# A gated mix of decode attention and an MLP: one row of w2 goes to 32 partitions in loads of six, with 29 products fewer on TensorE

## The chip, the cores and the metric

The kernel runs on one core of a Trainium2 chip, all in 32-bit floats. The metric is the device time of one execution in microseconds. Before the change it is 721.7 us, the median of three runs (721.61 to 721.78).

## The reference

One decode step for two sequences (B = 2): a gate mixes attention over a cache of 4096 keys with a two-layer MLP. `x` is 2 x 576, `wq` 576 x 4096 (32 heads of 128), `wo` 4096 x 576, `w1` 576 x 4608, `w2` 4608 x 576.

```python
g = _sigmoid((x * gate_w).sum(-1, keepdims=True))
q = (x @ wq) as (B, 32 heads, 1, 128)
scores = einsum("bhqd,bhkd->bhqk", q, k_cache) * 128 ** -0.5
a = einsum("bhqk,bhkd->bhqd", softmax(scores), v_cache) as (B, 1, 4096) @ wo
b = gelu(x @ w1 + b1) @ w2 + b2
return g * a + (1 - g) * b
```

Nearly all of the 309 MB that are read are the two caches (2 x 134 MB); the four weight matrices are 40 MB. Each weight is used for two rows of x only, so the work is to bring the bytes in and to have each of them consumed in time.

## The kernel before

**The ring.** One SBUF tile of 3 slots, each 64 KB on all 128 partitions, receives every large load in a fixed order: `wq`, `w1`, then for each of 16 units (one sequence, four heads) a K tile and a V tile, and last three slots of weights. `load()` takes the next load from a list and issues it from SP; `load_next(what)` notes that a slot has been read and issues what may follow. The list `LAST` says which rows of `w2` and `wo` are in the last three slots: rows 0 to 27 of `w2` in the first, rows 28 to 35 of `w2` and 0 to 14 of `wo` in the second, the rest of `wo` in the third, in pieces that get smaller. `w2` and `wo` are laid out so that partition p holds rows 36p to 36p + 35 of `w2` (32p to 32p + 31 of `wo`); "row r" below is row r of each partition, and a product with it contracts over the 128 partitions.

**A unit of attention.** VectorE multiplies the K tile by q (`mul`), GpSimd and VectorE sum it up (`red`), VectorE finds the maximum, ScalarE makes the exponentials (`softmax`), and TensorE multiplies them with the V tile (`av`), one unit behind. The K slot is free for the next load when VectorE has read it, the V slot when `av` is done.

**The end.** While the last unit is in work, the rows of `w2` are multiplied with the MLP's hidden values `hg` into an accumulator `acc` (`mlp_out`, `acc_mm`: the columns go in two halves of 288, a product each), then rows of `wo` with the normed attention output `oP` (`wo_out`). A product in 32-bit floats is two passes of TensorE, so the profile counts two matmuls for each. From row `FOLD` of `wo` on, products go to a second accumulator `res` in quarters of 144 columns (`part`), and `acc` is copied to SBUF and folded into `res` by four small products (L473). So the copy of `acc` and the fold are out of the way while the last pieces of `wo` come in. Two copies and one output DMA end the program.

**Row 35 of w2.** Its last 384 columns are loaded apart (`"wx"` in `LAST`): the 128 partitions' pieces go to 16 partitions, eight pieces of 384 columns each, by four loads. Load c goes to partitions c, c + 4, c + 8 and c + 12. Row 35's hidden values are brought to the same places by eight small products (`hxps`, L417), and `mlp_x` multiplies the eight pieces, two products for each.

**The start.** `xps` transposes x by column groups, once for the order of rows in which `w1` is loaded (two chunks of two rows per partition) and once for that of `wq` (four rows). `zps` sums x times the gate's weights by five products. Then come q's products (`qps`) and, behind them, the hidden layer's (`hps`).

Of the kernel before, what the change touches and what calls it, by code (L numbers as in the profile page):

```python
# [10 lines left out]
ALU = mybir.AluOpType  # L11
AX = mybir.AxisListType
P = 128
# [6 lines left out]
def kernel(  # L20
# [14 lines left out]
    nc = tc.nc  # L35
    B, H, SK, DH = k_cache.shape
    D = x.shape[-1]
    F = w1.shape[1]
    NX = D // P
# [9 lines left out]
    ROWS = {"wq": (4,), "w1": (2, 2)}  # L49
# [8 lines left out]
    NF = F // P  # L58
# [5 lines left out]
    SLOTS = 3  # L64

    LAST = (
        (("w2", 0, 14), ("w2", 14, 28)),
        (("w2", 28, 36), ("wx", 0, 1), ("wo", 0, 15)),
        (("wo", 15, 23), ("wo", 23, 27), ("wo", 27, 30), ("wo", 30, 31), ("wo", 31, 32)),
    )  # L70
    FOLD = 23
    SLOT = R * DH
    ALIGN = 512
    FREE0 = 16512
# [24 lines left out]
    kt, vt, wqt, w1t, rows = {}, {}, {}, {}, {}  # L99
# [9 lines left out]
    def load_w(w, rows, c):  # L109
        if c < len(rows):  # L110
            n = rows[c] * w.shape[1]
            lo = sum(rows[:c]) * P
            src = w[lo:lo + rows[c] * P].rearrange("(p r) n -> p (r n)", r=rows[c])
        else:
            n = w.shape[1] // 2
            src = w[NX * P:].rearrange("q (e n) -> (q e) n", e=2)
        t = ring[:, used["w"]:used["w"] + n]
        used["w"] += n
        nc.sync.dma_start(t, src)
        return t  # L120
# [11 lines left out]

    srcs = {"w2": w2.rearrange("(p r) n -> p (r n)", r=NF), "wo": wo.rearrange("(p r) n -> p (r n)", r=32)}

    XE, XC, XW = 4, 4, 384
    XL = D - XW
    XP = XE * XC
    XS = P // XP
    srcx2 = w2.rearrange("(e c s r) n -> c r e s n", e=XE, c=XC, s=XS)[:, NF - 1, :, :, XL:]

    def length(w, a, z):
        return XS * XW if w == "wx" else (z - a) * D - (XW if (w, z) == ("w2", NF) else 0)

    def load_last(m):
        n = sum(length(*q) for q in LAST[m])

        used["e"], used["z"] = len(held) % SLOTS * SLOT + n, (len(held) % SLOTS + 1) * SLOT
        t = slot(n)
        o = 0
        for w, a, z in LAST[m]:  # L150
            if w == "wx":
                xt = t[:XP, o:o + XS * XW]
                rows[w] = xt.rearrange("p (s n) -> p s n", s=XS)
                o += XS * XW
                for c in range(XC):
                    nc.sync.dma_start(xt[c::XC].rearrange("e (s n) -> e s n", s=XS), srcx2[c])
                continue
            if (w, z) == ("w2", NF):
                nc.sync.dma_start(t[:, o:o + length(w, a, z)], srcs[w][:, a * D:z * D - XW])
                for r in range(a, z):  # L160
                    rows[w, r] = t[:, o + (r - a) * D:o + min((r - a + 1) * D, length(w, a, z))]
                o += length(w, a, z)
                continue

            ends = (a * D, a * D + DS, a * D + DS + DO, z * D) if (w, z) == ("wo", 32) else (a * D, z * D)
            for u, v in zip(ends, ends[1:]):
                nc.sync.dma_start(t[:, o:o + v - u], srcs[w][:, u:v])
                o += v - u
            for r in range(a, z):
                rows[w, r] = t[:, o - (z - r) * D:o - (z - r - 1) * D]  # L170

    def temp(n, parts=P):
        t = ring[:parts, used["t"]:used["t"] + n]
        used["t"] += n
        assert used["t"] <= SLOTS * SLOT
        return t
# [30 lines left out]
    xg = temp(D, B + 1)  # L207
# [22 lines left out]
    ident = cp.tile([P, P], F32, name="ident")  # L230
# [29 lines left out]
    nc.gpsimd.memset(xe, 0.0)  # L260
    for e in range(2):
        nc.scalar.copy(xe[:, e, e::2], xg[:, NX * P:])
    def x_rows(rows):
        ends = [sum(rows[:c]) * P for c in range(len(rows) + 1)]
        return [xg[:, lo + r:hi:n] for n, lo, hi in zip(rows, ends, ends[1:]) for r in range(n)]

    srcx = x_rows(ROWS["w1"]) + [xe[:, 0], xe[:, 1]] + x_rows(ROWS["wq"])
    NXT = len(srcx)
    xps = ps_sm.tile([P, NXT, 4], F32, tag="sm", name="xps")
    for c, src in enumerate(srcx):  # L270
# [4 lines left out]
    gT = temp(NX + 1)  # L275
    nc.scalar.copy(gT, xps[:, :NX + 1, B])

    zps = ps_sm.tile([P, B], F32, tag="sm", name="zps")
    for c in range(NX + 1):
        nc.tensor.matmul(zps, gT[:, c:c + 1].to_broadcast([P, P]), xT[:, c, :B], start=(c == 0), stop=(c == NX))  # L280
    gb = cp.tile([P, B], F32, name="gb")
    g1 = cp.tile([P, B], F32, name="g1")
    nc.scalar.activation(gb, zps, AF.Exp, scale=-1.0)  # L283
# [5 lines left out]
    def proj(w, ts, banks, width):  # L289
        full = NG * len(banks) * width  # L290
        for c, n in enumerate(ROWS[w] + (1,)):
            last = c == len(ROWS[w])
            for r in range(n):
                k = sum(ROWS[w][:c]) + r
                for m, ps in enumerate(banks):
                    for j in range(NG):
                        o = (j * len(banks) + m) * width
                        if last:
                            e, o = divmod(o, full // 2)
                            lhs = xT[:, NX + e]  # L300
                        else:
                            o += r * full
                            lhs = xT[:, k if w == "w1" else NX + 2 + k]
                        nc.tensor.matmul(  # L304
                            ps[32 * j:32 * j + 32, :width], lhs, ts[c][:, o:o + width], start=(k == 0), stop=last,
                            skip_group_check=True,
                        )
# [56 lines left out]
    def acc_mm(lhsT, rhs, k, start=False, stop=False, lo=0):  # L364
        m = lhsT.shape[-1]
        hi = lo + rhs.shape[-1]
        for s in range(NS):
            o = 64 * (k % 2) + 32 * s
            u, v = max(lo, s * DS), min(hi, (s + 1) * DS)
            if u < v:  # L370
                nc.tensor.matmul(  # L371
                    acc[o:o + m, u - s * DS:v - s * DS], lhsT, rhs[:, u - lo:v - lo],
                    start=start, stop=stop, skip_group_check=True,
                )
# [39 lines left out]

    hxps = ps_sm.tile([XP, XS, B], F32, tag="sm", name="hxps")
    for s in range(XS):
        nc.tensor.matmul(  # L417
            hxps[:, s], ident.rearrange("p (q s) -> p s q", s=XS)[:, s], hg[:, NF - 1], start=True, stop=True
        )
    hx = cp.tile([XP, XS, B], F32, name="hx")  # L420
    nc.scalar.copy(hx, hxps)

    def mlp_x():
        for s in range(XS):
            acc_mm(hx[:, s], rows["wx"][:, s], s, lo=XL)

    def mlp_out(lo, hi):
        for r in range(lo, hi):
            acc_mm(hg[:, r], rows["w2", r], r)
# [19 lines left out]
    def last_out():  # L449
        res = ps_big.tile([32 * (NC - 1) + B, DO], F32, tag="big", name="res")  # L450
        sums = late(DS)
        nc.scalar.copy(sums, acc)

        def half(t, s):
            if s < 2:
                return t[:, s * DO:(s + 1) * DO]
            return t.rearrange("p (q g c) -> p g q c", q=2, g=2)[:, s - 2]

        def cols(row, s):
            return half(row[:, s // 2 * DS:(s // 2 + 1) * DS], s)  # L460

        def part(r, s):
            nc.tensor.matmul(  # L463
                res[32 * s:32 * s + B], oP[:, :, r], cols(rows["wo", r], s),
                start=r == FOLD, stop=r == 31, skip_group_check=True,
            )

        for r in range(FOLD, 31):
            for s in range(NC):
                part(r, s)  # L470
            if r == FOLD + 3:
                for s in range(NC):
                    nc.tensor.matmul(  # L473
                        res[32 * s:32 * s + B], fold[:, s // 2], half(sums, s),
                        start=False, stop=False, skip_group_check=True,
                    )

        osb = late(D, B)
        cpy = (nc.vector.tensor_copy, nc.scalar.copy)
        for s in range(2):  # L480
            part(31, s)
        for s in range(2):
            cpy[s](osb[:, s * DO:(s + 1) * DO], res[32 * s:32 * s + B])  # L483
        DW = DO // 2
        for q in range(2):
            for s in range(2, NC):
                nc.tensor.matmul(
                    res[32 * s:32 * s + B, q * DW:(q + 1) * DW], oP[:, :, 31], cols(rows["wo", 31], s)[:, q],
                    start=False, stop=True, skip_group_check=True,
                )  # L490
        for s in range(2, NC):
            cpy[s - 2](cols(osb, s), res[32 * s:32 * s + B].rearrange("p (q c) -> p q c", q=2))
        nc.sync.dma_start(out.rearrange("b s d -> (b s) d"), osb)
# [96 lines left out]
    for i in range(N):  # L590
        k = i - 1
# [31 lines left out]
    mlp_out(18, 20)  # L623
    norm_t()
    o_turn(turn)
    mlp_out(20, 24)
    mlp_x()
    mlp_out(24, NF)
    wo_out(0, FOLD)
    last_out()  # L630

# [27 lines left out]
```

## Time and profile before

| | |
|---|---|
| median of three runs | 721.7 us |
| the profiled execution: span from the first to the last instruction | 719.7 us |
| TensorE, matmul passes | 223.4 us busy (31%), 1663 |
| VectorE | 512.0 us busy (71%) |
| GpSimd | 145.0 us busy (20%) |
| ScalarE | 40.0 us busy (6%) |
| DMA from SP's queue | 99.2% of 16 engines' span, 308.55 MB |

The profile gives no other time for its own execution than the span; the 2.0 us between it and the median lie around the first and the last instruction. Engine times are summed over instructions of very different stages. A share of busy time says little by itself: the chain of waits and the windows of a stretch tell what a stage waits for.

### The profile page before, as it was taken

The page shows a single profiled execution, that of the slowest core. Times are in us where ns is not written, and L with a number is a line of the kernel's source. Part 1 is how long each engine was busy: PE and PEld are TensorE (multiplying, and loading weights), DVE is VectorE, ACT ScalarE, POOL GpSimd, SP SyncE. Part 2 cuts the span into 40 slices and gives each one's busy share as a digit, 9 for nine tenths or more (in the row PEclk, how much of TensorE's full clock was granted, in tenths as well). Part 3 has the DMA queues.
Part 4 walks back from the last instruction along what each step waited for, and adds up shares of the span by engine and source line. Part 5 has one row for each costly group of instructions (what it writes and reads, how often), then busy time and mean ns, then how long its engine had stood idle before and what let it go on. Part 6 is the DMA issues. An engine that isn't in the chain of part 4 may idle for free.

```text
span 719.7 us, 3913 instructions
## 1 busy us (share of the span) xinstructions
PE 223.4 (31%) x1663; PEld 66.1 (9%) x1663; DVE 512.0 (71%) x137; ACT 40.0 (6%) x156; POOL 145.0 (20%) x35
## 2 busy tenths in 40 slices
PE   0675022040514050404133140405060503214198
PEld 0321000010101010101000010101010100000024
DVE  0004969779695969596969879696959695988910
ACT  0110010100001010101010100001010101010000
POOL 2000130404050403022040404040403122040400
PEclk9967557565757575655756575757565665657588
DMA  9999999999999999999999999999999999999997
GB/s 408 412 443 434 426 444 419 455 416 455 416 444 428 426 441 430 438 430 444 430 434 426 441 430 437 431 433 437 437 434 441 423 431 437 430 441 431 420 424 308
DMA packets 7126, 308.83 MB, mean 429 GB/s; under 512 B 810, under 2 KB 1342, under 8 KB 1604
## 3 DMA queue, kind: packets, MB, share of 16 engines
q1 hardware_dynamic: 7060, 308.55, 99.2%
q8 instruction: 13, 0.21, 0.1%
q14 instruction: 5, 0.04, 0.0%
q10 hardware_dynamic: 48, 0.03, 0.0%
HBM read 308.57 MB, written 0.00 MB: 429 GB/s over the span
## 4 chain that ended last, share of the span: by engine, by line
DMA 45%; DVE 35%; PE 17%; ACT 1%; issue 1%; ACTq 0%; POOL 0%; DVEq 0%; POOLq 0%
DMA ring<-in_A_k_cache_dram 39%; DVE ring L512 19%; PE av L551 10%; DVE s L517 10%; DVE s L518 5%; DMA ring<-in_B_w_dram 4%; PE acc L371 3%; DMA ring<-in_gate_w_dram 3%; PE oall L568 2%; PE qps L304 1%; DVE avs L562 1%; PE res L463 0%; ACT p L537 0%; DVE m L522 0%; PE zps L280 0%
## 5 line engine op out<-in xcount | busy, mean ns | idle before, releaser
L512 DVE TENSOR_TENSOR ring<-ring,q 128x16384 f32<-128x16384 f32 x16 | 275.6, 17225 | 110.1 <-DMA ring<-in_A_k_cache_dram 110.1
L516 POOL TENSOR_TENSOR ring<-ring 128x3968 f32<-128x3968 f32 x16 | 137.0, 8565 | 491.3 <-DVE ring L512 491.3
L551 PE MATMUL av<-ring,p 128*32 128x512 f32 x1024 | 141.6, 715 | 167.6 <-ACT p L537 167.6
L517 DVE TENSOR_REDUCE s<-ring 128x66 f32<-128x8448 f32 x16 | 143.2, 8953 | 1.3
L568 PE MATMUL oall<-avs,pick 128*64 128x512 f32 x16 | 14.8, 1028 | 195.1 <-DVE avs L562 167.7
L518 DVE TENSOR_REDUCE s<-ring 128x62 f32<-128x3968 f32 x16 | 68.4, 4277 | 0.1
L551 PEld LDWEIGHTS av<-ring,p 128*32 128x32 f32 x1024 | 36.0, 129 | 278.8 <-issue 220.6
L537 ACT ACTIVATE p<-s,bs 32x128 f32<-32x128 f32 x64 | 25.5, 398 | 479.9 <-DVE bs L531 478.7
L352 PE MATMUL qb<-qm,spread 64*128 64x512 f32 x8 | 8.3, 1138 | 71.4 <-POOL qm L348 71.4
L395 DVE TENSOR_TENSOR ring<-hps,ring 128x384 f32<-128x384 f32 x3 | 1.7, 559 | 32.2 <-PE hps L304 32.0
L371 PE MATMUL acc<-ring,hg 128*2 128x288 f32 (+1 forms) x142 | 14.4, 561 | 25.3 <-DMA ring<-in_B_w_dram 25.3
L568 PEld LDWEIGHTS oall<-avs,pick 128*64 128x64 f32 x16 | 2.2, 196 | 201.9 <-DVE avs L562 201.9
L284 DVE TENSOR_SCALAR gb<-gb 128x2 f32<-128x2 f32 x1 | 0.2, 169 | 24.4 <-ACT gb L283 24.4
L483 DVE COPY ring<-res 2x144 f32<-2x144 f32 x1 | 0.3, 296 | 19.3 <-PE res L463 19.3
L304 PE MATMUL hps<-ring 128*32 128x384 f32 x120 | 12.8, 596 | 0.0
L562 DVE TENSOR_TENSOR avs<-av,selr 128x512 f32<-128x512 f32 x8 | 5.5, 682 | 10.1 <-PE av L551 10.1
L348 POOL TENSOR_TENSOR qm<-qall,mine 64x512 f32<-64x512 f32 x4 | 4.1, 1035 | 40.3 <-ACT qall L331 40.3
L537 ACT ACTIVATION_READ_ACCUMULATOR p<-s,bs 32x1 f32 x64 | 11.8, 184 | 0.0
L304 PE MATMUL qps<-ring 128*32 128x512 f32 x80 | 10.7, 697 | 0.0
L271 PE MATMUL xps<-ident,ring 3*128 3x3 f32 x10 | 1.5, 254 | 23.8 <-DMA ring<-in_gate_w_dram 22.8
L352 PEld LDWEIGHTS qb<-qm,spread 64*128 64x128 f32 x8 | 2.0, 308 | 74.5 <-POOL qm L348 74.5
L354 ACT COPY q<-qb 128x512 f32<-128x512 f32 x4 | 2.3, 585 | 106.3 <-PE qb L352 106.3
(88 smaller groups left out, 79.5 us busy)
## 6 DMA issues: line engine op xcount, KB each, us to landing
ring<-in_B_w_dram SPq DMA_DIRECT2D x2, 4608.0 KB, 34.3
ring<-in_B_w_dram SPq DMA_DIRECT2D x2, 4032.0 KB, 28.6
ring<-in_A_wo_dram SPq DMA_DIRECT2D x1, 4320.0 KB
ring<-in_A_wo_dram SPq DMA_DIRECT2D x1, 2304.0 KB, 22.4
ring<-in_B_w_dram SPq DMA_DIRECT2D x1, 2112.0 KB
ring<-in_B_w_dram SPq DMA_DIRECT2D x1, 1152.0 KB
ring<-in_A_wo_dram SPq DMA_DIRECT2D x1, 1152.0 KB
ring<-in_A_wq_dram SPq DMA_DIRECT2D x1, 1024.0 KB
```

What stands on the lines that cost most here:

```text
L304: nc.tensor.matmul(ps[32 * j:32 * j + 32, :width], lhs, ts[c][:, o:o + width], start=(k == 0), stop=last, skip_group_check=True,)
L348: nc.gpsimd.tensor_mul(t, qall.unsqueeze(1).to_broadcast([NO, NQ, DH]), mine[:, u[0]:u[-1] + 1].unsqueeze(2).to_broadcast([NO, NQ, DH]),)
L352: nc.tensor.matmul(ps, spread, t.rearrange("p u d -> p (u d)"), start=True, stop=True)
L371: nc.tensor.matmul(acc[o:o + m, u - s * DS:v - s * DS], lhsT, rhs[:, u - lo:v - lo], start=start, stop=stop, skip_group_check=True,)
L512: nc.vector.tensor_mul(kt[i], kt[i], qs[i].unsqueeze(1).to_broadcast([P, R, DH]))
L516: nc.gpsimd.tensor_add(t[:, :, :DH2], t[:, :, :DH2], t[:, :, DH2:])
L517: nc.vector.tensor_reduce(st[i][:, HALVED:], kt[i][:, HALVED:], AX.X, ALU.add)
L518: nc.vector.tensor_reduce(st[i][:, :HALVED], t[:, :, :DH2], AX.X, ALU.add)
L537: nc.scalar.activation(p[w, :, e * RB:(e + 1) * RB], st[i][w].rearrange("p (t c) -> p t c", c=RB), AF.Exp, bias=bias[i][w], accum_out=rs[w ...
L551: nc.tensor.matmul(ps[32 * j:32 * j + 32], p[:, 32 * t + EB * (1 - half):32 * t + EB * (1 - half) + 32], vt[i][:, RB * t:RB * (t + 1)].rea ...
L562: nc.vector.tensor_mul(t, avs[i].rearrange("p (r d) -> p r d", d=DH), selr.unsqueeze(2).to_broadcast([P, RB, DH]))
L568: nc.tensor.matmul(oall, pick[:, NO - G - i * G:2 * NO - G - i * G], avs[i].rearrange("p r d -> p (r d)"), start=(i == 0), stop=(i == N // ...
```

## The change

Row 35 of `w2` goes whole (576 columns) to 32 partitions: partition q gets four pieces, those of w2's partitions q, q + 32, q + 64 and q + 96, at a step of 768 columns. It is loaded by six loads of up to six neighbouring partitions, three behind rows 0 to 13 and three behind rows 14 to 21, all in the first slot; rows 22 to 34 move to the second. The hidden values of row 35 take four small products instead of eight, and `mlp_x` eight full-width products instead of sixteen narrow ones. The second accumulator begins at row 27 of `wo`, and the fold stands behind row 29. At the start, both weights are taken in the order of four rows per partition, so x is transposed once (6 transposes instead of 10), and the gate's sum is a multiply and a reduction on VectorE and one product.

```diff
     LAST = (
-        (("w2", 0, 14), ("w2", 14, 28)),
-        (("w2", 28, 36), ("wx", 0, 1), ("wo", 0, 15)),
+        (("w2", 0, 14), ("wx", 0, 3), ("w2", 14, 22), ("wx", 3, 6)),
+        (("w2", 22, 35), ("wo", 0, 15)),
...
-    FOLD = 23
+    FOLD = 27
...
-            lo = sum(rows[:c]) * P
-            src = w[lo:lo + rows[c] * P].rearrange("(p r) n -> p (r n)", r=rows[c])
+            lo = sum(rows[:c]) * w.shape[1]
+            src = w[:NX * P].rearrange("(p r) n -> p (r n)", r=NX)[:, lo:lo + n]
...
-    XE, XC, XW = 4, 4, 384
-    XL = D - XW
-    XP = XE * XC
+    XE, XP = 6, 32
     XS = P // XP
-    srcx2 = w2.rearrange("(e c s r) n -> c r e s n", e=XE, c=XC, s=XS)[:, NF - 1, :, :, XL:]
+    XT = 768
+    srcx2 = w2.rearrange("(s q r) n -> q s r n", q=XP, s=XS)[:, :, NF - 1]
...
-                for c in range(XC):
-                    nc.sync.dma_start(xt[c::XC].rearrange("e (s n) -> e s n", s=XS), srcx2[c])
...
+                for c in range(a, z):
+                    u, v = c * XE, min((c + 1) * XE, XP)
+                    nc.sync.dma_start(rows[w][u:v], srcx2[u:v])
...
-    srcx = x_rows(ROWS["w1"]) + [xe[:, 0], xe[:, 1]] + x_rows(ROWS["wq"])
+    srcx = [xg[:, r:NX * P:NX] for r in range(NX)] + [xe[:, 0], xe[:, 1]]
...
-    for c in range(NX + 1):
-        nc.tensor.matmul(zps, gT[:, c:c + 1].to_broadcast([P, P]), xT[:, c, :B], start=(c == 0), stop=(c == NX))
+    xz = temp((NX + 1) * B).rearrange("p (b c) -> p b c", b=B)
+    nc.vector.tensor_mul(
+        xz, xT[:, :NX + 1, :B].rearrange("p c b -> p b c"), gT.unsqueeze(1).to_broadcast([P, B, NX + 1])
+    )
+    zs = temp(B)
+    nc.vector.tensor_reduce(zs, xz, AX.X, ALU.add)
+    nc.tensor.matmul(zps, ones.to_broadcast([P, P]), zs, start=True, stop=True)
...
-        nc.tensor.matmul(
-            hxps[:, s], ident.rearrange("p (q s) -> p s q", s=XS)[:, s], hg[:, NF - 1], start=True, stop=True
-        )
+        nc.tensor.matmul(hxps[:, s], ident[:, s * XP:(s + 1) * XP], hg[:, NF - 1], start=True, stop=True)
...
-            acc_mm(hx[:, s], rows["wx"][:, s], s, lo=XL)
+            acc_mm(hx[:, s], rows["wx"][:, s], s)
...
-            if r == FOLD + 3:
+            if r == FOLD + 2:
...
-    mlp_out(20, 24)
+    mlp_out(20, 22)
     mlp_x()
-    mlp_out(24, NF)
+    mlp_out(22, NF - 1)
```

SP's queue, from the last V tile's load to the first of `wo` (names are out<-in, sizes partitions x elements), before:

```order
L130 DMA ring<-in_A_v_cache_dram 128x16384
L167 DMA ring<-in_B_w_dram 128x8064 x2
L159 DMA ring<-in_B_w_dram 128x4224
L156 DMA ring<-in_B_w_dram 4x8x384 x4
L167 DMA ring<-in_A_wo_dram 128x8640
```

and after:

```order
L130 DMA ring<-in_A_v_cache_dram 128x16384
L163 DMA ring<-in_B_w_dram 128x8064
L157 DMA ring<-in_B_w_dram 6x4x576 x3
L163 DMA ring<-in_B_w_dram 128x4608
L157 DMA ring<-in_B_w_dram 6x4x576 x2
L157 DMA ring<-in_B_w_dram 2x4x576
L163 DMA ring<-in_B_w_dram 128x7488
L163 DMA ring<-in_A_wo_dram 128x8640
```

The small loads moved from behind the second slot's `w2` into the first slot, between and behind its two parts, and part of the first slot's rows moved to the second.

TensorE, from the end of the attention (`op_t` turns its output) to the end of the program, before (the pairs of `hx` products of 96 and 288 columns, eight in all, are cut to the last):

```order
L441 MATMUL op_t<-ring 128x64
L371 MATMUL acc<-ring,hg 2x288 x8
L371 MATMUL acc<-ring,hx 2x96
L371 MATMUL acc<-ring,hx 2x288
L371 MATMUL acc<-ring,hg 2x288 x22
L371 MATMUL acc<-ring,hg 2x192
L371 MATMUL acc<-ring,oP 2x288 x46
L463 MATMUL res<-ring,oP 2x144 x16
L473 MATMUL res<-ring,fold 2x144 x4
L463 MATMUL res<-ring,oP 2x144 x18
L487 MATMUL res<-ring,oP 2x72 x4
```

and after:

```order
L436 MATMUL op_t<-ring 128x64
L368 MATMUL acc<-ring,hg 2x288 x4
L368 MATMUL acc<-ring,hx 2x288 x8
L368 MATMUL acc<-ring,hg 2x288 x26
L368 MATMUL acc<-ring,oP 2x288 x54
L458 MATMUL res<-ring,oP 2x144 x12
L468 MATMUL res<-ring,fold 2x144 x4
L458 MATMUL res<-ring,oP 2x144 x6
L482 MATMUL res<-ring,oP 2x72 x4
```

The sixteen `hx` products became eight, four rows of `wo` moved from `res` to `acc`, and the fold now has only six quarter products and the last four behind it.

More of the change, by code (lines that the diff above doesn't have):

```diff
@@ L133 @@
     srcs = {"w2": w2.rearrange("(p r) n -> p (r n)", r=NF), "wo": wo.rearrange("(p r) n -> p (r n)", r=32)}
-    XE, XC, XW = 4, 4, 384
-    XL = D - XW
-    XP = XE * XC
+    XE, XP = 6, 32
     XS = P // XP
-    srcx2 = w2.rearrange("(e c s r) n -> c r e s n", e=XE, c=XC, s=XS)[:, NF - 1, :, :, XL:]
+    XT = 768
+    srcx2 = w2.rearrange("(s q r) n -> q s r n", q=XP, s=XS)[:, :, NF - 1]
     def length(w, a, z):
-        return XS * XW if w == "wx" else (z - a) * D - (XW if (w, z) == ("w2", NF) else 0)
+        if w == "wx":
+            return XS * XT if a == 0 else 0
+        return (z - a) * D
     def load_last(m):
@@ L151, in load_last @@
             if w == "wx":
-                xt = t[:XP, o:o + XS * XW]
-                rows[w] = xt.rearrange("p (s n) -> p s n", s=XS)
-                o += XS * XW
-                for c in range(XC):
[L156 to L161, printed above, removed]
+                if a == 0:
+                    rows[w] = t[:XP, o:o + XS * XT].rearrange("p (s n) -> p s n", s=XS)[:, :, :D]
+                for c in range(a, z):
+                    u, v = c * XE, min((c + 1) * XE, XP)
+                    nc.sync.dma_start(rows[w][u:v], srcx2[u:v])
                 o += length(w, a, z)
@@ L262 @@
         nc.scalar.copy(xe[:, e, e::2], xg[:, NX * P:])
-    def x_rows(rows):
-        ends = [sum(rows[:c]) * P for c in range(len(rows) + 1)]
-        return [xg[:, lo + r:hi:n] for n, lo, hi in zip(rows, ends, ends[1:]) for r in range(n)]
-    srcx = x_rows(ROWS["w1"]) + [xe[:, 0], xe[:, 1]] + x_rows(ROWS["wq"])
+    srcx = [xg[:, r:NX * P:NX] for r in range(NX)] + [xe[:, 0], xe[:, 1]]
     NXT = len(srcx)
@@ L302, in proj @@
                             o += r * full
-                            lhs = xT[:, k if w == "w1" else NX + 2 + k]
+                            lhs = xT[:, k]
                         nc.tensor.matmul(
```

## The prediction

> **What bounds the kernel now.** I read the page first: its header, the row of DMA busy shares in 40 slices, and the chain of work that ended last.
>
> ```profile
> span 719.7 us, 3913 instructions
> DMA  9999999999999999999999999999999999999997
> DMA packets 7126, 308.83 MB, mean 429 GB/s; under 512 B 810, under 2 KB 1342, under 8 KB 1604
> DMA 45%; DVE 35%; PE 17%; ACT 1%; issue 1%; ACTq 0%; POOL 0%; DVEq 0%; POOLq 0%
> ```
>
> The span is 2.0 us below the median of the three runs (721.7 us); the profile gives no other time of its own, so every sum is made on the span and the 2.0 us are added back. All 16 DMA engines are at 90% or more in every slice but the last: 308.83 MB at 429 GB/s are 719.9 us, the span itself. The chain names TensorE and VectorE for half of the time, but it only walks through whoever consumed a tile last. So I read the end closely: first the windows (last two columns: mean busy share of the 16 DMA engines, GB/s), then the timeline of the last 2 us.
>
> ```profile
> 691.00:695.00 4.00, 4.00 (x44) 1.11 (x36) 1.21 (x4) 0.16 (x1) 0.00 (x0) 1.00 1.05 439
> 700.00:712.00 12.00, 12.00 (x134) 5.11 (x126) 0.00 (x0) 0.00 (x0) 0.00 (x0) 0.68 0.97 415
> 713.10:713.70 0.60, 0.60 (x15) 0.19 (x8) 0.00 (x0) 0.00 (x0) 0.00 (x0) 1.00 0.84 332
> 713.70:714.30 0.60, 0.60 (x20) 0.39 (x16) 0.00 (x0) 0.14 (x1) 0.00 (x0) 1.00 0.81 329
> 714.30:714.90 0.60, 0.60 (x28) 0.47 (x18) 0.00 (x0) 0.27 (x1) 0.00 (x0) 1.00 0.63 231
> 714.90:715.50 0.60, 0.60 (x21) 0.31 (x15) 0.00 (x0) 0.00 (x0) 0.00 (x0) 1.00 0.63 228
> 715.50:716.10 0.60, 0.60 (x28) 0.47 (x20) 0.00 (x0) 0.00 (x0) 0.00 (x0) 1.00 0.47 152
> 716.10:716.40 0.30, 0.30 (x14) 0.08 (x4) 0.00 (x0) 0.00 (x0) 0.00 (x0) 1.00 0.21 63
> 716.40:716.70 0.30, 0.30 (x10) 0.11 (x7) 0.00 (x0) 0.00 (x0) 0.00 (x0) 1.00 0.00 0
> ...
> 714.93 0.09 PEld L473 LDWEIGHTS res<-ring,fold 128*2 128x2 f32 x2
> 715.25 0.84 PEld L463 LDWEIGHTS res<-ring,oP 128*2 128x2 f32 x32 [0.23 <-DMA ring<-in_A_wo_dram]
> 716.32 0.10 PEld L463 LDWEIGHTS res<-ring,oP 128*2 128x2 f32 x4 [0.23 <-DMA ring<-in_A_wo_dram]
> 716.55 0.28 PEld L487 LDWEIGHTS res<-ring,oP 128*2 128x2 f32 x8
> ```
>
> Two things are to be seen. The engines do not stop together: the share falls from 0.84 to 0.00 over 3.3 us, so some have done their part by 713.7 and the last work until 716.4. And TensorE, behind until 714.93, waits for wo's last pieces at 715.25 and 716.32. The end is therefore the landing of wo's last piece on the slowest engine, with some 3.3 us of products, copies and output write behind it that the change leaves alone. The idle share below 1 from 713.1 to 716.4, 0.6 x (0.16 + 0.19 + 0.37 + 0.37 + 0.53) + 0.3 x 0.79, is 1.2 us: no rebalancing of engines that moves the same bytes can bring more than that.
>
> **TensorE's part.** The groups of the last 30 us, two pieces of the timeline, one of the chain of waits (zps) and one of SP's timeline:
>
> ```profile
> L371 PE MATMUL acc<-ring,oP 128*2 128x288 f32 x92 | 6.5, 406 | 0.0
> L463 PE MATMUL res<-ring,oP 128*2 128x144 f32 x68 | 3.0, 286 | 0.0
> ...
> 698.94 4.01 PE L371 MATMUL acc<-ring,hx 16*2 16x96 f32 x32
> 702.88 0.66 PE L371 MATMUL acc<-ring,hg 128*2 128x288 f32 x4
> ...
> 25.71 2.26 PE zps L280 x10
> 36.96 0.33 SPq L130 DMA_DIRECT2D ring<-in_A_k_cache_dram  x1
> ```
>
> A product is two passes, so x32 are 16 products. Row 35's slices: 16 products from 698.94 to 702.88, 3.94 us; 8 of them at full width remain, about 2 us by halving; the product with 192 columns goes too (0.25 us by the same pace). wo's rows 23 to 26: 16 products less at 3.0/34 = 0.09 us, 8 more at 6.5/46 = 0.14 us, 0.3 us less. In sum 2.5 us less work for TensorE, all ahead of the waits at 715.25 and 716.32 and hidden by them. Against it, the products that fold in the accumulator move behind row 29, past the wait at 715.25. They are 8 passes at 3.0/68 = 0.04 us, 0.35 us, where 0.23 us are idle before 716.32; the 0.1 us that may be left is absorbed by the next pieces of wo. Sum: 0.
>
> At the start 4 transposes, 4 products of the gate and 4 of hxps go, and VectorE gets a multiply and a reduction, for which TensorE waits ahead of q's products. Four fifths of 2.26 us are 1.8 us less, two short VectorE operations some 0.5 us more; so the first K load, at 36.96, goes out about 1.3 us earlier, and even if it went out later the queue ahead of it is full (the second and third slices read 9). w1 is fetched in the same pieces of two rows, from places twice as far apart. No row prices that; between 0 and the slowest slice's pace I take 0, since the same number of bytes per piece is fetched.
>
> **The queue's part, which decides.** An engine's pace is 429/16 = 26.8 KB per us. Row 35's 192 columns leave the loads over all 128 partitions: 8 partitions x 768 B = 6.1 KB per engine, -0.23 us. The small loads grow from 4 x 48 KB to 288 KB, so the bytes in all stay as they are and only their places change. If a partition's bytes stay on one engine (taken, since a load of few partitions has no finer share that any row shows), four engines had 48 KB each, 1.83 us; now a partition gets 9 KB, 0.34 us, four engines carry five of these (1.72 us) and two carry six (2.06 us). Net of the -0.23 us: 0.0 us for the two, -0.3 us for two others that had such loads before, +1.5 us for two that had none, -0.23 us for the ten others. If the bytes spread over all engines, all get 0. So by bytes alone the last landing moves by 0.0 to -0.23 us.
>
> But the loads also change where engines write. Before, a load stepped by 4 partitions: partitions c, c+4, c+8, c+12. Now six neighbours are written by six engines at once. The window 691 to 695 shows the four old loads in passing at 439 GB/s, no slower than the stretch behind them: with a step of 4 they disturb nobody. No row shows engines writing neighbours at one time, so I bound it. Low end: 0, an engine's pace is its own. [...] The engines are not quite in step: they are spread over 3.3 us at the end, and a load reached alone costs only its 0.34 us. I take the middle, 2.7 us: of the two ends the nearer row is the spread, and it is of the length of the loads themselves. The loads stand some 8 to 20 us into the first slot's transfers, on full queues, so nothing later makes up for it. With 0.2 us of it met by what these engines shed, the last landing is 2.5 us later: 721.7 + 2.5 = 724.2 us.
>
> [...]
>
> **SP's queue and the second slot.** SP's timeline, and one of its waits (us in total, times, longest):
>
> ```profile
> 651.58 3.76 SPq L167 DMA_DIRECT2D ring<-in_B_w_dram  x2
> 681.63 0.33 SPq L159 DMA_DIRECT2D ring<-in_B_w_dram  x1
> 682.39 2.84 SPq L156 DMA_DIRECT2D ring<-in_B_w_dram  x4
> 689.74 0.33 SPq L167 DMA_DIRECT2D ring<-in_A_wo_dram  x1
> ...
> SPq L167 <- DMA ring<-in_B_w_dram: 5.9, 2, 4.6
> ```
>
> The second slot is issued at 681.63, when VectorE is done with the last K tile; that does not move. Ahead of it the first slot now holds 22 rows of w2, not 28: 6 x 2,304 B x 128 = 1.77 MB, 4.1 us less in every engine. The issue at 689.74 ended the 4.6 us wait, for rows 14 to 27 to land, so the slowest engine's queue reached 8.1 us past 681.63 and now reaches 4.0 us past it, and the fastest, 3.3 us ahead, 0.7 us. The six small loads add 1 us to their own engines there. An empty queue took 1.0 us from issue to first packet:
>
> ```profile
> 0.74 0.87 SPq L119 DMA_DIRECT2D ring<-in_A_wq_dram  x2
> ...
> 0.70:1.70 1.00, 0.00 (x0) 0.00 (x0) 0.00 (x0) 0.00 (x0) 0.97 (x1) 1.00 0.00 0
> 1.70:2.20 0.50, 0.00 (x0) 0.00 (x0) 0.00 (x0) 0.00 (x0) 0.42 (x3) 1.00 4.25 1442
> ```
>
> So the earliest engines may idle for about 0.3 to 1 us, and they have that to spare at the end. Term: 0, high end +1 us. The small loads cost SP 0.6 to 0.8 us each to issue; two more fit into the wait before 681.63.
>
> **Rivals.** (1) Engines do not share a way: only bytes count, 721.7 - 0.2 = 721.5 us. For it: no row shows a slow-down between engines. Against it: all 16 together sit at one ceiling slice after slice (429 GB/s), which fits a limit at the destination as well as one in the engine. From 1.4 us of meeting upwards it loses to the forecast; between 0.2 and 1.4 us the result is within the bound too. (2) TensorE's chain is what counts and 29 products fewer shorten it: at most 2.5 us, 719.2 us; but only if the landings came earlier by as much, and balance can give 1.2 us, so 720.5 us. Against it are the waits at 715.25 and 716.32. (3) The two engines that are new to the small loads are among the last: the last landing comes 1.5 us later, 723.2 us; they would have to be of the few that work past 715.5 (share 0.47). (4) The queue runs dry for the slow engines as well: an issue would have to take 4 us and more to reach them; 721.7 + 1.5 = 723.2 us.
>
> **How the numbers follow.** The forecast, meeting with more than 1.4 us, has 0.55, its own range 723.2 to 725.6 us; meeting with less 0.10; rival 1 0.28; rival 2 0.02; rivals 3 and 4 together 0.05. A difference under 0.2% (1.4 us) is about what a measurement of this kernel cannot tell from no change. Faster: 0.02 of rival 2 and 0.01 for an unforeseen gain, 0.03; slower: 0.55 + 0.04 (the half of the 0.05 that tops the bound, and unforeseen losses), 0.59; same: 0.38. The range goes from rival 1's 721.4 us to 725.5 us, short of the 727.0 us of engines fully in step.
>
> **What would show it.** In the windows of the stretch 677 to 690 us the GB/s should dip below 400 while the busy share stays near 1, and the last landing (the last wait of the weight loads for wo, now near 716.6) should come near 719. Right on TensorE: longer idle time before the last products. Wrong if the small loads pass at 420 GB/s or more and the share falls to zero by 716.5: then rival 1 holds. A dip of the share itself near 682 to 684 us would be rival 4.

## The result: 724.2 us, 0.35% slower, and the profile after

The changed kernel takes 724.24 us (median of five runs, 723.88 to 724.70), the kernel before beside it 721.70 us (721.61 to 721.86): a ratio of 1.0035, 95% interval 1.0023 to 1.0047. So it is slower by 2.5 us, with 54 matmul passes fewer. From the page:

```profile
span 722.6 us, 3811 instructions
PE 213.5 (30%) x1609; PEld 59.4 (8%) x1609; DVE 512.3 (71%) x139; ACT 40.0 (6%) x156; POOL 144.9 (20%) x35
DMA packets 7141, 308.82 MB, mean 427 GB/s; under 512 B 826, under 2 KB 1230, under 8 KB 1620
DMA 49%; DVE 35%; PE 14%; ACT 1%; issue 1%; ACTq 0%; DVEq 0%; POOL 0%; POOLq 0%
```

The bytes are the same to 0.01 MB, and TensorE is busy 9.9 us less. The chain of work that ended last has lost three points of TensorE and gained four of DMA. Now the end, in the same windows as before (from 713.1 us; last two columns: mean busy share of the 16 DMA engines, GB/s):

```profile
713.10:713.70 0.60, 0.60 (x16) 0.29 (x11) 0.00 (x0) 0.00 (x0) 0.00 (x0) 1.00 0.99 415
713.70:714.30 0.60, 0.60 (x18) 0.47 (x12) 0.00 (x0) 0.00 (x0) 0.00 (x0) 1.00 0.94 390
714.30:714.90 0.60, 0.60 (x16) 0.43 (x10) 0.00 (x0) 0.00 (x0) 0.00 (x0) 1.00 1.00 405
714.90:715.50 0.60, 0.60 (x12) 0.09 (x2) 0.00 (x0) 0.00 (x0) 0.00 (x0) 1.00 0.93 363
715.50:716.10 0.60, 0.10 (x6) 0.05 (x8) 0.00 (x0) 0.00 (x0) 0.00 (x0) 1.00 0.73 271
716.10:716.70 0.60, 0.60 (x12) 0.28 (x16) 0.00 (x0) 0.00 (x0) 0.00 (x0) 1.00 0.60 230
716.70:717.30 0.60, 0.51 (x12) 0.00 (x0) 0.00 (x0) 0.03 (x1) 0.00 (x0) 1.00 0.51 175
717.30:717.90 0.60, 0.00 (x0) 0.00 (x0) 0.00 (x0) 0.38 (x1) 0.00 (x0) 1.00 0.19 66
717.90:718.50 0.60, 0.40 (x16) 0.36 (x20) 0.00 (x0) 0.00 (x0) 0.00 (x0) 1.00 0.10 35
718.50:719.10 0.60, 0.60 (x31) 0.52 (x23) 0.00 (x0) 0.00 (x0) 0.00 (x0) 1.00 0.07 22
719.10:719.70 0.60, 0.60 (x28) 0.43 (x16) 0.00 (x0) 0.00 (x0) 0.00 (x0) 1.00 0.01 3
```

And the timeline of TensorE's weight loads there (start, us, what, in brackets the idle time before it):

```profile
713.30 1.69 PEld L368 LDWEIGHTS acc<-ring,oP 128*2 128x2 f32 x32 [0.25 <-DMA ring<-in_A_wo_dram]
716.05 0.59 PEld L368 LDWEIGHTS acc<-ring,oP 128*2 128x2 f32 x16 [1.06 <-DMA ring<-in_A_wo_dram]
718.10 0.60 PEld L458 LDWEIGHTS res<-ring,oP 128*2 128x2 f32 x24 [1.45 <-DMA ring<-in_A_wo_dram]
```

The windows hold two losses of different kinds. First, everything is later: from 714.3 to 714.9 us all engines still work (1.00) where before 0.63 did. The share summed over these windows is 0.6 x 6.07 = 3.64 us, against 0.6 x 3.38 + 0.3 x 0.21 = 2.09 us in the rows of before. So the average engine ends 1.55 us later, with no byte more in all, and the engines without small loads are among these: six of 16 alone would be a share of 0.375. Second, the tail is longer: from 717.9 to 719.1 us the share is 0.10 and then 0.07, and one engine of 16 is 0.0625. One engine works alone for about 1 us, and the last landing moves from about 716.5 to about 719.1 us, by 2.6 us. TensorE, the weight loads show, now waits 1.06 and 1.45 us for `wo` where it waited 0.23 us twice.

The stretch in which the small loads are fetched, before and then after:

```profile
677.00:680.00 3.00, 0.00 (x0) 0.00 (x0) 2.88 (x2) 0.00 (x0) 0.28 (x1) 0.50 1.02 441
680.00:685.00 5.00, 4.78 (x52) 1.61 (x56) 2.29 (x4) 1.96 (x8) 0.00 (x0) 0.63 1.00 432
685.00:690.00 5.00, 5.00 (x56) 1.44 (x48) 0.00 (x0) 0.00 (x0) 0.00 (x0) 1.00 0.96 410
```

```profile
677.00:680.00 3.00, 0.02 (x3) 0.02 (x6) 2.88 (x2) 0.00 (x0) 0.29 (x1) 0.50 0.99 382
680.00:685.00 5.00, 5.00 (x52) 1.66 (x56) 2.30 (x4) 1.96 (x8) 0.00 (x0) 0.61 1.03 387
685.00:690.00 5.00, 5.00 (x54) 1.44 (x48) 0.00 (x0) 0.06 (x1) 0.00 (x0) 1.00 1.00 361
690.00:700.00 10.00, 8.49 (x83) 2.46 (x79) 2.63 (x9) 0.37 (x1) 0.00 (x0) 0.88 1.00 428
```

The share stays at 1 while the rate falls to 361 to 387 GB/s: packets take longer. That is 3 x 59 + 5 x 45 + 5 x 49 = 647 KB short of before, 1.5 us of the whole core at 429 GB/s.

### The profile page after: what moved, and what is told of

Read it like the earlier page. It is cut to its first block, busy times and chain, and to the rows that moved or that the text cites. A ratio compares the mean times of both kernels' runs of the same rounds, so it can differ in the third digit from the quotient of the medians.

```text
span 722.6 us, 3811 instructions
## 1 busy us (share of the span) xinstructions
PE 213.5 (30%) x1609; PEld 59.4 (8%) x1609; DVE 512.3 (71%) x139; ACT 40.0 (6%) x156; POOL 144.9 (20%) x35
## 4 chain that ended last, share of the span: by engine, by line
DMA 49%; DVE 35%; PE 14%; ACT 1%; issue 1%; ACTq 0%; DVEq 0%; POOL 0%; POOLq 0%
DMA ring<-in_A_k_cache_dram 39%; DVE ring L507 19%; DVE s L512 10%; PE av L546 9%; DVE s L513 5%; DMA ring<-in_A_wo_dram 4%; DMA ring<-in_B_w_dram 4%; DMA ring<-in_gate_w_dram 3%; PE oall L563 2%; PE qps L301 1%; PE acc L368 1%; DVE avs L557 1%; ACT p L532 0%; DVE m L517 0%; DVE mt L522 0%
## 5 line engine op out<-in xcount | busy, mean ns | idle before, releaser
L546 PE MATMUL av<-ring,p 128*32 128x512 f32 x1024 | 135.9, 691 | 171.5 <-ACT p L532 171.5
L368 PE MATMUL acc<-ring,hg 128*2 128x288 f32 x140 | 13.9, 548 | 24.9 <-DMA ring<-in_B_w_dram 24.9
L368 PE MATMUL acc<-ring,oP 128*2 128x288 f32 x108 | 8.7, 475 | 2.9 <-DMA ring<-in_A_wo_dram 2.9
```

The source lines that it names most:

```text
L368: nc.tensor.matmul(acc[o:o + m, u - s * DS:v - s * DS], lhsT, rhs[:, u - lo:v - lo], start=start, stop=stop, skip_group_check=True,)
L546: nc.tensor.matmul(ps[32 * j:32 * j + 32], p[:, 32 * t + EB * (1 - half):32 * t + EB * (1 - half) + 32], vt[i][:, RB * t:RB * (t + 1)].rea ...
```

## Experiments

Three causes are told apart. **N**: small loads to neighbouring partitions slow each other. **Q**: large loads are issued so late that queues run dry. **L**: one of the two engines that are new to the small loads is a late one and decides by its bytes. The experiments ran in three groups of four, each on one chip with the kernel before beside it, at 721.73, 721.68 and 721.78 us.

**The parts that the prediction put at 0.** The kernel before with only the start part of the change (its diff as it stands) and the later fold:

```diff
-    FOLD = 23
+    FOLD = 27
...
-            if r == FOLD + 3:
+            if r == FOLD + 2:
```

> The kernel before with only the start part of the change (w1's pieces, 4 transposes and 4 products fewer, VectorE's multiply and sum) and the later fold (row 27, added behind row 29); row 35 and its loads as before. All theories, and the prediction's terms of 0 for these parts: 721.5 to 721.9 us. If the work that TensorE loses mattered, 720.5 us; if the fold behind row 29 or the wait for VectorE cost something, 722.0 us or more.

Measured: 721.92 us (721.75 to 721.99, 11 runs), ratio 1.0000 (0.9992 to 1.0009). These parts neither cost nor bring anything that can be measured; the whole loss belongs to row 35, its loads and the shorter first slot that goes with them.

**Neighbours alone.** The kernel before, its four small loads sent to four neighbours each:

```diff
-    srcx2 = w2.rearrange("(e c s r) n -> c r e s n", ...)[:, NF - 1, :, :, XL:]
+    srcx2 = w2.rearrange("(c e s r) n -> c r e s n", ...)[:, NF - 1, :, :, XL:]
...
-                    nc.sync.dma_start(xt[c::XC].rearrange("e (s n) -> e s n", s=XS), srcx2[c])
+                    nc.sync.dma_start(xt[c * XE:(c + 1) * XE].rearrange("e (s n) -> e s n", s=XS), srcx2[c])
```

> The kernel before (721.7 us), but load c of row 35's slices goes to partitions 4c to 4c + 3 instead of c, c + 4, c + 8, c + 12; bytes, engines, queue places and products are the same. N: slower, by 1 to 5 us (four loads that take up to 1.8 us each where 0.46 us were due), 722.7 to 727 us, with a dip of the GB/s in the window 691 to 695 us (439 before). Q and L: 721.7 us, no change.

Measured: 722.87 us (722.71 to 723.39, 11 runs), ratio 1.0016 (1.0008 to 1.0025). The same bytes in the same number of issues, on as many engines, cost 1.1 us more. In the windows:

```profile
690.00:695.00 5.00, 5.00 (x52) 1.57 (x48) 0.71 (x2) 0.43 (x1) 0.00 (x0) 1.00 1.04 410
717.30:717.90 0.60, 0.60 (x22) 0.20 (x12) 0.00 (x0) 0.00 (x0) 0.00 (x0) 1.00 0.08 23
```

The loads pass at 410 GB/s (436 in the same window before), and an engine is at work past 717.3 us. N is shown. The expectation's 1.8 us for each of the four loads, 7.3 us where 1.83 us were due, was the author's estimate for four engines that go one after another; no run shows it, and 1.1 us came. That the place of writing is what counts stays an inference: neighbours are also fetched from places closer together, and no run parted the two.

**The loads left out.** The changed kernel without the six loads and their products (`pass` in place of the `dma_start`, no `mlp_x()`).

> The changed kernel without the six small loads and without the eight products on them; row 35 of w2 is left out of the result, and 288 KB are not read. The first slot is as short as in the changed kernel, so its queues are as dry. N and L: the whole loss goes and 0.2 us more, 721.3 to 721.6 us, GB/s near 420 in the window 685 to 690 us. Q: 722.5 us and more, and the dip stays.

Measured: 721.92 us (721.53 to 724.08, 11 runs), ratio 1.0007 (0.9998 to 1.0015). So by the medians the loads are 2.3 of the 2.5 us. But the windows, of an execution of 723.1 us, warn:

```profile
677.00:680.00 3.00, 0.00 (x0) 0.00 (x0) 2.90 (x2) 0.00 (x0) 0.58 (x1) 0.50 0.89 381
680.00:685.00 5.00, 4.94 (x48) 1.58 (x52) 2.58 (x4) 1.96 (x8) 0.00 (x0) 0.57 1.02 395
685.00:690.00 5.00, 5.00 (x57) 1.53 (x52) 0.00 (x0) 0.00 (x0) 0.00 (x0) 1.00 0.93 387
```

The rate dips to 381 to 395 GB/s there without any small load. In two of the rows the share is 0.89 and 0.93: the shortened first slot leaves early engines idle, as Q says. In the middle row it is 1.02 at 395 GB/s, so packets are slow there too. By the median this costs 0.4 us against the 721.5 us that the shed bytes alone would give. It also brings a wider scatter: the slowest execution, at 724.08 us, takes as long as the changed kernel. The dip in this stretch, which the prediction named as its mark, is therefore no proof of N.

**The loads moved elsewhere.** Two runs take the first slot as before and put the six loads behind. In the first they stand behind `w2`'s row 34, ahead of `wo`:

```diff
-        (("w2", 0, 14), ("wx", 0, 3), ("w2", 14, 22), ("wx", 3, 6)),
-        (("w2", 22, 35), ("wo", 0, 15)),
+        (("w2", 0, 14), ("w2", 14, 28)),
+        (("w2", 28, 35), ("wx", 0, 6), ("wo", 0, 15)),
```

> The changed kernel, but with the first slot as before (w2's rows 0 to 27) and all six small loads in the second slot behind rows 28 to 34, where the kernel before has its four. Q: the loss by dry queues goes, 722.5 to 723 us. N and L: the loss stays, 724.0 to 724.8 us, and the dip of the GB/s moves to the stretch behind 690 us.

Measured: 724.31 us (723.72 to 724.79, 6 runs), ratio 1.0034 (1.0022 to 1.0046). In the second they stand behind `wo`'s row 14 as well (`("w2", 28, 35), ("wo", 0, 15), ("wx", 0, 6)`, and `mlp_x()` between `wo_out(0, 15)` and `wo_out(15, FOLD)`):

> The changed kernel with w2's rows 0 to 27 in the first slot, and in the second rows 28 to 34, then wo's rows 0 to 14, and the six small loads of 6 neighbours last; TensorE takes the 8 products of row 35 behind wo's row 14. So no large load is issued late: wo's first piece follows at 682, not at 689.5 as where six small loads stood ahead of it, and the first slot is as long as before. Theory Q in its wider form (a large load issued when the engines are about to run out slows all of them): 722.8 to 723.5 us, what is left being neighbours and the late engine. Theories N and L without Q: 724.0 to 724.6 us, as the changed kernel.

Measured: 724.76 us (724.65 to 725.01, 5 runs), ratio 1.0040 (1.0026 to 1.0054). The rows of the windows, of the first and then of the second:

```profile
690.00:695.00 5.00, 4.58 (x48) 1.31 (x40) 1.60 (x4) 0.00 (x0) 0.00 (x0) 1.00 1.20 377
695.00:700.00 5.00, 3.14 (x27) 0.96 (x27) 1.03 (x5) 0.00 (x0) 0.00 (x0) 0.68 0.88 344
```

```profile
690.00:695.00 5.00, 5.00 (x50) 1.43 (x43) 0.69 (x1) 0.43 (x1) 0.00 (x0) 1.00 1.04 447
695.00:700.00 5.00, 3.50 (x50) 1.54 (x52) 1.95 (x8) 0.00 (x0) 0.00 (x0) 1.00 1.01 432
700.00:705.00 5.00, 2.09 (x32) 0.69 (x24) 0.00 (x0) 0.00 (x0) 0.00 (x0) 1.00 1.02 342
705.00:712.00 7.00, 5.86 (x64) 2.19 (x68) 0.00 (x0) 0.00 (x0) 0.00 (x0) 0.76 0.96 368
```

The dip goes where the loads go: to 690 to 700 us, then to 700 to 712 us, where before moved 412 and 416 GB/s. In the second run that is 5 x 70 + 7 x 48 = 686 KB, 1.6 us of the whole core, at a share near 1. Its first slot is as long as before. The first piece of the third slot was issued later, at 694.4 us and not at 688.1, but the share shows no empty queue, so dry queues have no part in its 3.0 us.

**A late issue alone.** In the first of these two runs SP issued `wo`'s first piece at 689.5 us instead of 685.3, since it waited for an earlier transfer to land. So the kernel before was given six issues for its four small loads, same bytes and places:

```diff
-                    nc.sync.dma_start(xt[c::XC]..., srcx2[c])
+                    for u, v in ((0, XS // 2), (XS // 2, XS)) if c < 2 else ((0, XS),):
+                        nc.sync.dma_start(xt[c::XC]...[:, u:v], srcx2[c][:, u:v])
```

> The kernel before, with two of its four small loads cut into halves by columns: same bytes on the same engines and partitions, a step of 4, only six issues for four. wo's first piece then waits for the landing of w2's rows 14 to 27 and is issued near 689.5 us and not at 685.3. Theory Q in its wider form: 722.2 to 723.0 us, with GB/s below 400 in 690 to 700. Theories N and L: 721.7 us, no dip.

Measured: 721.63 us (721.50 to 721.95, 11 runs), ratio 0.9997 (0.9988 to 1.0006). One row of SP's timeline, then two of the windows:

```profile
689.72 0.34 SPq L170 DMA_DIRECT2D ring<-in_A_wo_dram  x1
```

```profile
690.00:695.00 5.00, 5.00 (x52) 1.53 (x48) 0.69 (x1) 0.15 (x1) 0.00 (x0) 1.00 1.03 426
695.00:700.00 5.00, 3.50 (x46) 1.52 (x46) 1.95 (x8) 0.28 (x1) 0.00 (x0) 0.85 1.03 444
```

The issue is late, and no dip and no loss follow: Q in its wider form, that a late issue alone costs time, falls. Where a late issue does cost is shown by accident. Row 35 on five engines, in seven loads (`slice(c, 30, 6) if c < 6 else slice(30, 32)`, in the second slot):

> Row 35 on five engines: six small loads of 5 partitions a step of 6 apart and one of 2, in the second slot; 54 KB for three engines and 63 KB for two of the old four. Theory L: if the late engine is the sixth, it is out of it, and 721.7 to 722.2 us; if it is the fifth, 722.8 us or more, as with six engines. Theory N: 721.5 to 721.9 us. This is also the smallest change that could give a version as fast as the kernel before with eight products of full width.

Measured: 725.45 us (724.87 to 727.76, 5 runs), ratio 1.0058 (1.0045 to 1.0071). A seventh issue made SP wait once more. Again one row of SP's timeline and two of the windows:

```profile
695.44 0.82 SPq L163 DMA_DIRECT2D ring<-in_A_wo_dram  x2
```

```profile
690.00:695.00 5.00, 5.00 (x52) 1.45 (x44) 1.11 (x4) 0.00 (x0) 0.00 (x0) 1.00 0.62 249
695.00:700.00 5.00, 3.49 (x35) 1.01 (x35) 1.53 (x6) 0.41 (x1) 0.00 (x0) 0.77 0.86 298
```

Here the share itself falls to 0.62: engines are empty. That is what rival 4 would look like, and the changed kernel shows nothing of the kind. About five engines and lateness this run says nothing.

**A step of 5.** The changed kernel, partition c + 5e in place of 6c + e (`q = slice(c, 30, 5) if c < 5 else slice(30, 32)`), first in the places of the change, then in the second slot:

> The changed kernel (724.24 us), but a small load goes to partitions c, c + 5, ... c + 25 instead of six neighbours (the last one to 30 and 31 as before): same engines, bytes, places in the queue. Theory N (engines of one load that write neighbouring partitions hold each other and the rest up): most of a slow-down of about 1.7 us goes, 722.4 to 723.0 us, and the GB/s of the window 685 to 690 us rise from 361 towards 420. Theory Q (the second slot is issued too late for the shortened first slot, queues run dry): nothing changes, 724.2 us. Theory L (one of the two engines that are new to the small loads is a late one): by itself also 724.2 us; together with N 722.8 us is left.

Measured: 723.43 us (five runs: 723.12, 723.43, 723.43, 725.02, 725.19), ratio 1.0032 (1.0020 to 1.0045).

> The changed kernel with both suspects but one taken away: six small loads to partitions a step of 5 apart (no neighbours) and behind w2's rows 28 to 34 in the second slot (no dry queue); the two engines that are new to small loads keep them. Theory N alone (neighbours are the loss): 721.5 us, as before. Theory L (one of the two new engines is late into w2 and decides by its bytes): 722.8 to 723.1 us, with the share of DMA time at 0.06 to 0.1 for the last 0.6 us or more. Theory Q (dry queue): 721.5 us.

Measured: 723.81 us (723.35, 723.51, 723.81, 725.58, 725.61), ratio 1.0037 (1.0025 to 1.0050). Neither differs from the changed kernel beyond the intervals, so both expectations missed: a step of 5 doesn't take the loss away. Both runs fall into two groups some 2 us apart, and the profiled executions (723.43 and 723.81 us) belong to the lower ones. In these, the share summed over the windows from 713.1 us on, as for the changed kernel, puts the average engine 0.85 and 0.98 us behind before, not 1.55: a part of the slow-down went.

A possible reason for the rest, only argued: the engines aren't in step (at the end of the kernel before they stop over 3.3 us, while a small load takes 0.34 us by the prediction's estimate), so one engine's load may meet another load of the engine that writes beside it. Why four loads with a step of 4, as in the next run, escape this, no run shows.

**Eight and four engines.** Row 35 in four loads with a step of 4, in the second slot: first on 32 partitions and eight engines (`q = slice(c, XP, 4)`, four loads), then on 16 partitions and four engines (`XE, XP = 4, 16`, `XT = 576`, so eight pieces per partition; rows 13 and 14 of `wo` move to the third slot).

> Row 35 on eight engines: four small loads of 8 partitions, a step of 4 apart, in the second slot; 36 KB per engine, so four engines get 1.15 us net that they had not, and the four old ones shed 0.7 us. Theory N: no neighbours, 721.5 us or below. Theory L: the late one is among the four new ones, 722.5 to 722.8 us, 0.2 to 0.4 us below six engines. Only the fullest engine counts: 721.2 us.

Measured: 722.53 us in two groups: 721.27, 721.33, 721.37, 721.53, and seven runs from 722.38 to 722.86; ratio 1.0007 (0.9999 to 1.0016).

> The whole of row 35 on four engines: four small loads of 4 partitions, a step of 4 apart, 18 KB each (8 products of 16 partitions), in the second slot; wo's rows 13 and 14 move to the third slot. The four engines get 72 KB where before they had 48, net of the 6 KB that every engine sheds +0.7 us for these; no neighbours and no engine new to small loads. Theory N: nothing beside the bytes, so 721.5 to 722.4 us, by how late the four are. Theory L: 722.4 us, since these four end within 0.6 us of the last engine before; still faster than six engines at a step of 5 though the loads per engine are larger. If neither counts and only the number of bytes in the fullest engine does (72 KB here, 54 KB with six), this is slower than six engines: 723.5 us or more against 722.9.

Measured: 722.57 us (722.47 to 722.76, 11 runs), ratio 1.0013 (1.0004 to 1.0022). Windows of the run on eight engines (its profiled execution belongs to the higher group), then of that on four:

```profile
690.00:695.00 5.00, 4.40 (x48) 1.42 (x36) 1.78 (x5) 0.00 (x0) 0.00 (x0) 1.00 1.06 443
695.00:700.00 5.00, 3.81 (x27) 1.13 (x27) 0.86 (x5) 0.41 (x1) 0.00 (x0) 0.64 1.00 431
715.50:716.10 0.60, 0.10 (x4) 0.10 (x8) 0.00 (x0) 0.07 (x1) 0.00 (x0) 1.00 0.35 111
716.10:716.70 0.60, 0.60 (x24) 0.53 (x23) 0.00 (x0) 0.00 (x0) 0.00 (x0) 1.00 0.06 23
716.70:717.30 0.60, 0.60 (x26) 0.51 (x20) 0.00 (x0) 0.00 (x0) 0.00 (x0) 1.00 0.05 15
```

```profile
716.10:716.70 0.60, 0.60 (x24) 0.52 (x28) 0.00 (x0) 0.00 (x0) 0.00 (x0) 1.00 0.23 76
716.70:717.30 0.60, 0.60 (x30) 0.50 (x20) 0.00 (x0) 0.00 (x0) 0.00 (x0) 1.00 0.23 55
```

The eight-engine run moves the same 288 KB as the change and shows no dip (443, 431): with a step of 4, N is gone. What is left is L, though no execution of the lower group was profiled. In the lower group the 721.4 us are those of bytes alone (721.7 less the shed 0.23). In the higher one a single engine (0.06, 0.05) works about 1.2 us past the others, and the groups lie 1.3 us apart (medians 722.68 and 721.35), which is 36 KB at 26.8 KB per us. On four engines 0.23 x 16 = 3.7 engines work to the end together: there the four carriers' 72 KB decide, in every run alike, at the 722.4 us that bytes give.

**Packet by packet.** The trace holds the size and the time of every packet, though no view prints them. One piece of row 35 is one packet. Undisturbed it takes 0.093 us (2,304 B), or 0.065 us in the kernel before (1,536 B). The last column adds up what all packets of `w2` and `wo` took beyond the time that the fastest twentieth of their size took.

| run | row 35's packets: mean, longest (us) | all packets: extra time per engine (us) |
|---|---|---|
| before (step of 4) | 0.065, 0.065 | 0.12 |
| neighbours alone | 0.085, 0.309 | 0.50 |
| the changed kernel | 0.119, 0.273 | 1.74 |
| the loads left out | none | 0.91 |
| neighbours behind `w2`'s row 34 | 0.134, 0.294 | 2.00 |
| neighbours behind `wo`'s row 14 | 0.130, 0.286 | 1.93 |
| step of 5: first slot, second slot | 0.105, 0.212 and 0.115, 0.271 | 0.97 and 1.15 |
| eight engines, step of 4 | 0.093, 0.093 | 0.15 |
| four engines, step of 4 | 0.093, 0.093 | 0.12 |

With a step of 4 not one of these packets is slowed; neighbours slow them and the full-width packets beside them, and a step of 5 slows them less. The run without the loads has slow packets too: 0.73 of its 0.91 us lie in rows 22 to 34 of `w2`, which come behind the shortened slot. In the changed kernel 0.99 of the 1.74 us lie in the same rows, which meet both the small loads and the short queue. No run parts the two there.

**One run that answered nothing.** The step of 5 behind `wo`'s row 14.

> The same with the six small loads a step of 5 apart: no neighbours, no late issue, only the bytes on six engines. Theory L: runs of two kinds, 722.6 to 723.1 us where a late engine is one of the six and 721.2 to 721.8 us where it is not. If L is nothing: 721.5 us in all runs. If the 723.8 us of the form with a step of 5 in the second slot ahead of wo came from bytes alone, and not from its late issue of wo: 723.5 us or more here.

Measured: 730.77 us (729.95 to 731.30, 4 runs). Two rows of its waits (us in total, times, longest):

```profile
ACT ring L615 <- DMA ring<-in_B_w_dram: 25.0, 1, 25.0
PEld op_t L436 <- ACT ring L615: 13.9, 1, 13.9
```

ScalarE's write of a small tile behind the stepped loads' place in the ring waited 25 us for them, and TensorE for ScalarE, so TensorE sets this time and not the transfers.

## Why the prediction came out

The total of 724.2 us was met, but as a sum of other terms than its own: one term came out smaller, and one that was left out of the sum made up for it. That the number fits so closely is luck.

- **What bounds the kernel** was right: the end is the landing of `wo`'s last piece on the slowest engine. TensorE lost work and only waits longer (1.06 and 1.45 us). Rival 2 falls with it, as does any cost of the fold: 721.92 us, ratio 1.0000, for those parts.
- **The start** was right at 0. In the timeline of the changed kernel, TensorE and then SP:

```profile
25.63 0.59 PE L277 MATMUL zps<-ring,ones 128*128 128x2 f32 x2 [0.85 <-DVE ring L276]
...
36.17 0.33 SPq L130 DMA_DIRECT2D ring<-in_A_k_cache_dram  x1
```

The gate's sum is now one product of 0.6 us, for which TensorE waits 0.85 us, and the first K load goes out 0.8 us earlier than at 36.96, not 1.3; the end does not move.
- **Neighbours, the term of +2.7 us**, was right in its sign and mis-sized. It was taken as the middle of two ends; the upper one, engines fully in step (727.0 us in all), was the author's estimate, and no run shows that end or the term. Alone in the kernel before, neighbours cost 1.1 us. Behind `wo`'s row 14, with no empty queue, the six loads take 1.6 us of the whole core; in the changed kernel at most 1.55 us, with the short queue's part in it. It was also put on too few engines: the prediction let only the six engines that carry small loads fall back. The windows show the average of all 16 engines 1.55 us later. Rival 1 falls.
- **Rival 3, a late carrier of small loads, is the rest**: one engine works alone for about 1 us at the end, and the run on eight engines, where no packet is slowed, falls into two groups 1.3 us apart. Rival 3 had a price of 1.5 us and shared a chance of 0.05 with rival 4. The step that failed is the condition "of the few that work past 715.5", with a share of 0.47 in that row: two new engines among 16, seven or eight of which work at 715.5, made it likely that one would be late, not unlikely. Single engines can be followed through the trace by the sizes and times of their packets: the engine that ends last carries small loads and began `w2` 1.0 us after the last of the others, in the changed kernel, and 0.9 us after in the higher group on eight engines. In the kernel before, and in both profiled executions with a step of 5 (lower groups), the engines that begin `w2` latest carry none. In the changed kernel the late carrier came on top of the neighbours instead of in their place: 1.55 + about 1.0 = 2.55 us, where 2.5 were measured (2.9 between the two profiled spans). The late carrier has five small loads, so by the prediction's count it is one of four engines, two of them new; that it is a new one is not shown, since the trace doesn't name the engines.
- **The dry queue, the term of 0 with +1 us above**, was a little low: without the loads 721.92 us, some 0.4 us over what bytes give. How much of the 1.55 us in the changed kernel is its part, no run shows; the run behind `wo`'s row 14 loses 3.0 us without empty queues. One reading behind this term was wrong: the wait that ended with the issue at 689.74 was 1.2 us long, and the one of 4.6 us ended at 694.77. The 8.1 us between 681.63 and 689.74 stand, so the term doesn't change.
- **The mark named for N**, a rate under 400 GB/s in 677 to 690 us, was seen and would have been seen without N too (381 to 395 with no small load). The share beside the rate doesn't part them either (1.02 at 395 GB/s). What told them apart was that the dip moved with the loads, and that a step of 4 took it away.

Open are three points: why one engine runs 1 us and more behind the others, and in which executions it is one of the carriers; whether neighbours collide where they are written or where they are read; and how the 1.55 us are split between neighbours and the short queue. No version with the whole of row 35 beats the kernel before: the nearest, eight engines with a step of 4, is at 1.0007 (0.9999 to 1.0016).

## What to carry to other kernels

When all DMA engines are busy to the end, count bytes per engine, not in all: here small loads on four engines left 3.7 engines at work to the end (share 0.23), and small loads on eight gave times 1.3 us apart (721.35 and 722.68 us), with one engine alone at the end of the slower ones (share 0.06, 0.05). Don't send the loads of one set to neighbouring partitions: here four loads with a step of 4 slowed no packet (0.093 us each), while neighbours (0.119 to 0.134 us on average) and, less so, a step of 5 (0.105 and 0.115 us) did. When a dip in the rate is to prove a cause, read the busy share beside it: here 249 GB/s at a share of 0.62 were engines without work, and 361 GB/s at a share of 1.00 slow packets, but the share did not tell why they were slow. Then move the suspect and see whether the dip follows.

## What the runs showed of the hardware

- Six small loads to neighbours, 288 KB, held up engines that carry none of them: the rate of the whole core fell from 412 to 342 GB/s for 5 us and from 416 to 368 for 7 us more, and the average engine ended 1.7 us later (the run behind `wo`'s row 14).
- The same 288 KB in four loads with a step of 4 slowed no packet: each of its packets of 2,304 B took 0.093 us, where the six loads to neighbours had 0.119 to 0.134 us on average.
- A load that SP issued 4.4 us later cost nothing (689.7 us, 721.63 us in all); one issued 10 us later came with 3.8 us more in all (695.4 us, 725.45 us, with row 35's bytes on five engines in it). In both, SP waited for an earlier load to land, with six and seven small loads ahead of the issue in place of four.
- With the same program, times fell into two groups 1.3 us apart (721.35 and 722.68 us). In the higher one an engine that began `w2` 0.9 us after the others carries small loads; that the lower one differs in this is inferred.
